# w_in's eight transfers held until unit 1's k has landed, in a kernel of a gated recurrence and a rational MLP

## The chip, the core and the metric

The kernel runs on one core of a Trainium2 chip. The metric is the device time of one execution in microseconds (us), lower is better. Engines are named as in the profile: PE (TensorE matmuls; PEld its weight loads), DVE (VectorE), ACT (ScalarE), POOL (GpSimd), SP (SyncE). SPq and POOLq are the queues from which SP and POOL issue DMAs.

## The reference, cut to what matters

Two computations in a row. First a gated linear recurrence for 4 batches, 8 heads, 768 time steps and a head size of 48; its output, laid out as 3072 tokens by 384, is the input x of an MLP with 2048 hidden units whose activation is a quotient of polynomials.

```python
f = 1.0 / (1.0 + np.exp(-f_logit))
for t in range(S):
    state = f[:, :, t, :, None] * state + np.einsum('bhd,bhe->bhde', k[:, :, t], v[:, :, t])
    y[:, :, t] = np.einsum('bhd,bhde->bhe', q[:, :, t], state)
...
h = x @ w_in
h2 = h * h
h3 = h2 * h
P = a[0] + a[1] * h + a[2] * h2 + a[3] * h3
Q = 1.0 + np.abs(b[0]) * np.abs(h) + np.abs(b[1]) * h2
g = P / (Q + 1e-06)
return (g @ w_out).astype(np.float32)
```

q, k, v and f_logit are float32 of shape (4, 8, 768, 48); w_in is 384 by 2048 and w_out 2048 by 384.

## The kernel before

The work is cut into 12 units. A unit is one batch and 256 time steps (`UB` = 2 blocks of 128 tokens); units 0 to 3 are the first 256 steps of the four batches, units 4 to 7 the next, and so on, so unit 4 needs the state that unit 0 leaves. Each unit goes through a recurrence part and an MLP part, and the parts of neighbouring units overlap.

The order of all work is written out by hand in the string `ORDER`. Each entry is a step, a call of a short function: `ld 1 k` calls `load(1, "k")`. The steps are issued in that order, and each engine and each DMA queue runs its own share of them strictly in order; semaphores between engines follow from the tiles that the steps read and write. So only the order within one engine or queue matters, and an instruction that waits holds up what stands behind it on its own engine. A number with `@` is one of four PSUM slots.

The steps that matter here (line numbers of the kernel before):

- `ld n f|k|q|v` (L204): loads f_logit, k, q or v of unit n. f, k and q go out on SP's queue, v on POOL's, where it is cast to bf16. Each of f, k, q is 128 partitions by 8 runs of 384 bytes, 1024 packets; unit 0's are split into halves. Each name has three buffers (`rings(key, 3, ...)`), so unit 3 uses unit 0's again.
- `wi m0 m1` (`load_w_in`, L212): loads columns m0*128 to m1*128 of w_in, cast to bf16, in four DMAs from POOL, one for each group of 32 partitions. `wi 0 8` and `wi 8 16` together are the whole matrix, eight DMAs of 192 KB. `wo` (L219) does the same for w_out.
- `ef`, `ls` (ACT, L282 and L287) make the log gates out of f; `cs` (PE, L297 and L302) sums them; `A` (ACT, L310) exponentiates; `xa n 1` and `xa n 0` (L315, on DVE, sometimes POOL) multiply k and q by that.
- `T` (PE, L329) transposes both, `Te` copies them out of PSUM (L336); `sc` (PE, L350) makes the scores, `mk` (DVE, L358) masks them; `vm` (POOL, L365) copies parts of v; `yi` and `yb` (PE, L371) form y; `ic`, `si` (PE, L417 and L426) and `st` (DVE, L446) carry the state; `ye` (ACT mostly, L434) writes x.
- `h n m0 m1` (PE, L455) is x @ w_in for hidden blocks m0 to m1, `hy` (ACT, L467) takes it out. `sq`, `ab`, `zv`, `p1`, `p2`, `pm`, `tv`, `gm` (DVE, L471 to L533), `lz`, `ex` (ACT, L501 and L506) and the accumulating DMAs `zd` (L497) and `ta` (L525) from POOL form g.
- `o` (PE, L542) is g @ w_out, `oe` (L548) takes it out into one of two buffers `osb`, `so` (L557, SP's queue, two DMAs) stores it.

Two suffixes tie a step to a DMA: `!w` puts a mark w on the step, and `^w` makes a step's instructions wait until what carries the mark is done (`behind`). Neither is used in the kernel before.

On POOL the first steps are `ld 0 v`, `ld 1 v`, `vm 0 1`, then the eight w_in DMAs, then `vm 0 0`, `ld 3 v`, `vm 1 1`, `vm 1 0`, `ld 2 v`. On SP's queue the loads go out in this order: unit 0's halves of f, k, q with unit 1's f among them, then `ld 2 f`, `ld 1 k`, `ld 1 q`, `ld 2 q`, `ld 3 f`, `ld 2 k`, `ld 4 f`, `ld 4 q`, `ld 3 q`.

Of the kernel before, what the change touches and what calls it, by code (L numbers as in the profile page):

```python
# [25 lines left out]
si 1 0 @3; ic 1; yi 0 1 @2; st 1 0; yb 0 2 4; Te 1; yb 0 0 2; ld 4 f; sc 1 0 @1; ye 0 s; ld 3 v; sc 1 1 @0
mk 1 0; si 1 1; vm 1 1; vm 1 0; h 0 0 4 @2; mk 1 1; ld 2 v; st 1 1; xa 2 0; h 0 4 8 @1; hy 0 0 4; ld 4 q
yi 1 1 @0; hy 0 4 8; yb 1 2 4; yb 1 0 2; ab 0 0 8; ef 3; h 0 12 16 @3; sq 0 0 8; ye 1 s; ld 3 q; ls 3
h 0 8 12 @2; zv 0 0 8; hy 0 12 16; cs 3 @1; xa 2 1; hy 0 8 12; h 1 4 8 @0; lz 0 0 8; ld 6 f; sq 0 8 16
h 1 8 12 @3; p1 0 0 16; ld 5 k; hy 1 4 8; si 2 0 @2; ab 0 8 16; A 3 0; T 2 @0; ld 3 k; pm 0 0 16; hy 1 8 12  # L30
Te 2 s; h 1 12 16 @3; ld 5 f; p2 0 0 16; ic 2; ld 5 q; ae 3; hy 1 12 16; h 1 0 4 @0; zv 0 8 16; ef 4; ta 0 8 16
ld 4 k; A 3 1; sc 2 0 @3; st 2 0; hy 1 0 4; xa 3 0; yi 2 1 @1; mk 2 0; xa 3 1 0 4 p; lz 0 8 16; sc 2 1 @0
si 2 1; mk 2 1; vm 3 1; ls 4; ic 3 @3; vm 2 1; st 2 1; vm 2 0; ex 0 0 16; ld 4 v; yb 2 2 4; sq 1 0 16; si 3 0
ta 0 0 8; yb 2 0 2; cs 4 @0; wo 12 16; ab 1 0 16; T 3 @2; wo 0 4; ae 4; vm 3 0; st 3 0; ye 2 s; wo 8 12
p1 1 0 16; si 3 1; A 4 1; h 2 0 4 @1; wo 4 8; Te 3 s; st 3 1; pm 1 0 16; h 2 4 8 @3; A 4 0; sc 3 0 @2; hy 2 4 8
u 1 12 16 @0; p2 1 0 16; hy 2 0 4; h 2 12 16 @3; ln 1 12 16; xa 4 0; ta 1 8 16; sc 3 1 @1; ef 5; mk 3 0
h 2 8 12 @0; xa 4 1 0 4 p; hy 2 12 16; mk 3 1; ls 5; yi 3 1 @2; yb 3 0 2; hy 2 8 12; gm 0 0 16; yb 3 2 4; ld 8 f
cs 5 @3; ye 3 s; ic 4 @1; ae 5; A 5 1; ab 2 0 16; h 3 8 12 @0; ef 6; A 5 0; zv 1 0 8; u 1 8 12 @2; hy 3 8 12
o 0 0 8 12 @3; sq 2 0 16; ln 1 8 12; si 4 0; h 3 4 8 @0; ls 6; lz 1 0 8; T 4 @2; p1 2 0 16; zd 2 0 8; o 0 1 0 4
st 4 0; xa 5 1 0 4 p; hy 3 4 8; Te 4; si 4 1; o 0 1 8 12; ex 1 0 16; st 4 1; sc 4 0 @0; ta 1 0 8; sc 4 1 @2  # L40
pm 2 0 16; o 0 0 12 16; zd 2 8 16; h 3 0 4 @1; ld 6 v; p2 2 0 16; o 0 0 4 8; ld 5 v; hy 3 0 4; o 0 1 4 8; ef 8
o 0 1 12 16; mk 4 1; ta 2 8 16; h 3 12 16 @1; lz 2 0 8; xa 5 0; o 0 0 0 4; vm 4 0; mk 4 0; vm 4 1; hy 3 12 16
yi 4 1 @2; yi 4 0; gm 1 0 16; yb 4 0 2; oe 0 0 2 s; yb 4 2 4; so 0 0 2; cs 6 @0; ye 4 s; ld 6 q; h 4 4 8 @1
ld 6 k; A 6 0; sq 3 0 16; lz 2 8 16; h 4 0 4 @3; ld 7 f; p1 3 0 16; ae 6; h 4 8 12 @2; hy 4 4 8; hy 4 0 4
ab 3 0 16; si 5 0 @1; ic 5; A 6 1; T 5 @3; tv 2 0 8; hy 4 8 12; zd 3 8 16; o 1 0 12 16 @0; st 5 0; ex 2 0 16
ld 7 q; o 1 0 0 4; pm 3 0 16; o 1 1 4 8; h 4 12 16 @2; ld 8 q; zv 3 0 8; o 1 0 4 8; hy 4 12 16; si 5 1
o 1 1 0 4; p2 3 0 16; o 1 1 12 16; Te 5 s; o 1 1 8 12; gm 2 0 16; ta 3 0 8; lz 3 8 16; ta 3 8 16; sc 5 1 @2
ld 7 k; sc 5 0 @3; o 1 0 8 12; vm 5 0; st 5 1; xa 6 1 0 4 p; ld 9 f; mk 5 1; o 2 0 0 4 @1; lz 3 0 8; o 2 1 12 16
mk 5 0; vm 5 1; ic 6 @2; vm 6 1; ls 8; sq 4 0 16; yi 5 0 @3; yi 5 1; oe 1 0 2 s; o 2 1 8 12; ef 7; o 2 0 4 8
ex 3 0 16; yb 5 0 2; xa 6 0; yb 5 2 4; o 2 1 4 8; ab 4 0 16; ld 8 v; si 6 0; o 2 0 12 16; p1 4 0 16; ld 7 v  # L50
T 6 @0; so 1 0 2; o 2 0 8 12; ld 8 k; ye 5 s; vm 6 0; st 6 0; zd 4 0 8; p2 4 0 16; ls 7; si 6 1; o 2 1 0 4
Te 6 s; h 5 12 16 @3; st 6 1; zv 4 8 16; cs 7 @2; oe 2 0 2 s; pm 4 0 16; h 5 0 4 @0; A 7 0; so 2 0 2; ld 10 f
hy 5 12 16; h 5 8 12 @1; hy 5 0 4; ld 11 f; gm 3 0 16; h 5 4 8 @3; ae 7; hy 5 8 12; A 7 1; sc 6 1 @0; xa 7 0
sc 6 0 @1; hy 5 4 8; cs 8 @2; mk 6 1; xa 7 1 0 4 p; lz 4 8 16; o 3 0 12 16 @3; o 3 0 8 12; mk 6 0; ta 4 0 8
T 7 @0; A 8 0; ab 5 0 16; ta 4 8 16; ld 9 k; ef 9; yi 6 1 @1; yi 6 0; o 3 1 8 12; sq 5 0 16; ae 8; A 8 1
o 3 0 4 8; Te 7 s; ld 9 q; yb 6 2 4; yb 6 0 2; p1 5 0 16; ic 7 @2; lz 4 0 8; sc 7 1 @0; si 7 0; o 3 1 4 8
ye 6 v; vm 8 0; vm 7 1; o 3 1 12 16; xa 8 1 0 4 p; ls 9; st 7 0; h 6 0 4 @1; mk 7 1; ex 4 0 16; zd 5 0 8; si 7 1
pm 5 0 16; h 6 4 8 @0; o 3 0 0 4; o 3 1 0 4; ld 10 k; vm 7 0; st 7 1; hy 6 0 4; xa 8 0; h 6 12 16 @2; ef 10
gm 4 0 16; h 6 8 12 @1; oe 3 0 2 s; hy 6 4 8; T 8 @3; zv 5 8 16; hy 6 12 16; so 3 0 2; sc 7 0 @0; hy 6 8 12
cs 9 @2; p2 5 0 16; ld 10 q; lz 5 8 16; o 4 1 8 12 @1; mk 7 0; o 4 0 8 12; ta 5 8 16; lz 5 0 8; ab 6 0 16  # L60
ta 5 0 8; yi 7 1 @0; yi 7 0; yb 7 0 2; ld 9 v; yb 7 2 4; Te 8; o 4 0 12 16; ye 7 s; vm 8 1; o 4 0 0 4; sq 6 0 16
A 9 0; o 4 1 4 8; A 9 1; sc 8 0 @3; ic 8 @0; ae 9; ex 5 0 16; sc 8 1 @2; xa 9 1 0 4 p; si 8 0; o 4 1 12 16
o 4 1 0 4; p1 6 0 16; zd 6 8 16; zd 6 0 8; ef 11; st 8 0; ld 10 v; mk 8 0; ls 10; h 7 4 8 @0; ls 11; mk 8 1
h 7 0 4 @3; xa 9 0; h 7 12 16 @2; hy 7 0 4; p2 6 0 16; hy 7 4 8; o 4 0 4 8; pm 6 0 16; h 7 8 12 @3; hy 7 12 16
cs 10 @0; hy 7 8 12; gm 5 0 16; yi 8 0 @2; ta 6 8 16; A 10 0; yi 8 1; yb 8 2 4; ae 10; yb 8 0 2; oe 4 0 2 s
T 9 @3; ye 8 s; so 4 0 2; sq 7 0 16; A 10 1; o 5 0 12 16 @1; ld 11 q; Te 9 s; si 9 0 @2; h 8 12 16 @0; ld 11 k
p1 7 0 16; o 5 0 0 4; hy 8 12 16; ic 9; ab 7 0 16; lz 6 0 8; sc 9 0 @3; sc 9 1 @0; o 5 0 4 8; tv 6 0 8
o 5 1 8 12; zd 7 0 8; lz 6 8 16; o 5 1 4 8; mk 9 1; xa 10 1 0 4 p; mk 9 0; h 8 4 8 @0; ex 6 0 16; vm 9 1
zd 7 8 16; xa 10 0; h 8 8 12 @3; vm 9 0; st 9 0; ld 11 v; p2 7 0 16; h 8 0 4 @2; pm 7 0 16; hy 8 8 12
o 5 1 12 16; o 5 1 0 4; hy 8 4 8; o 5 0 8 12; hy 8 0 4; cs 11 @3; gm 6 0 16; ta 7 8 16; oe 5 0 2 s; ic 10 @0  # L70
ta 7 0 8; A 11 0; yi 9 0 @2; yi 9 1; yb 9 2 4; A 11 1; sq 8 0 16; yb 9 0 2; ae 11; T 10 @1; ye 9 s; lz 7 0 8
si 10 0; h 9 8 12 @3; xa 11 0; ab 8 0 16; h 9 4 8 @2; hy 9 8 12; lz 7 8 16; p1 8 0 16; h 9 12 16 @3; zd 8 0 8
vm 10 0; st 10 0; vm 10 1; hy 9 4 8; Te 10; vm 11 0; o 6 0 12 16 @0; zd 8 8 16; o 6 1 4 8; hy 9 12 16; pm 8 0 16
sc 10 0 @2; ex 7 0 16; sc 10 1 @1; o 6 1 0 4; o 6 1 12 16; mk 10 0; xa 11 1 0 4 p; h 9 0 4 @3; mk 10 1
# [26 lines left out]
def kernel(  # L101
# [95 lines left out]
    def load(n, what, a0=0, a1=HP, qu="s"):  # L197
# [6 lines left out]
        return eng.dma_start(out=s[what][:, hh].rearrange("p h i d -> p h (i d)"),  # L204
                      in_=src[s["b"], hh, t0:t0 + NT, :].rearrange("h (p i) d -> p h (i d)", i=2))
# [404 lines left out]
```

## Time and profile before

| | |
|---|---|
| time, median of 3 runs | 233.66 us (233.58 to 235.81) |
| the profiled execution's own time | 234.32 us |
| its span, first to last instruction | 232.6 us |
| PE / DVE / ACT / POOL busy | 197.3 / 204.8 / 195.9 / 85.2 us |
| w_in's DMAs issued | from 8.97 us, 4.43 us for all eight |
| unit 1's k issued | at 6.66 us, its issue took 2.80 us |
| DVE's longest idle stretch | 5.67 us, ended by the landing of unit 1's k |

The times of instructions count from the start of the span. The row of a DMA instruction is its issue on the queue, not the transfer; when the data is there is seen in the landing, and in when a waiting instruction starts. What a row has in brackets is the idle time of the engine ahead of it and what ended it.

### The profile page before, as it was taken

To read this page: it belongs to the slowest core of one execution; us is meant where nothing else is said; L and a number is where in the kernel's file an instruction comes from. 1 tells how busy PE (TensorE), PEld (TensorE's weight loads), DVE (VectorE), ACT (ScalarE), POOL (GpSimd) and SP (SyncE) were. 2 spreads that over 40 slices of the span, in tenths; PEclk is the share of its full clock that TensorE was granted. 3 is DMA by queue.
4 is the path that set the end of the run, shared out by engine and by line. 5 is a ranking of instruction groups with operands and counts; after the bars stand their busy time and mean duration, and the time that the engine had idled before them with its cause. 6 is when DMAs were issued, how large, how long until landed. Compare 5 with 4: busy or idle time off the path is not lost.

```text
span 232.6 us, 6998 instructions
## 1 busy us (share of the span) xinstructions
PE 197.3 (85%) x3109; PEld 143.0 (61%) x3112; DVE 204.8 (88%) x184; ACT 195.9 (84%) x183; POOL 85.2 (37%) x104
## 2 busy tenths in 40 slices
...
DVE  5261788999999999999999999999999999979960
...
GB/s 143 220 233 232 260 179 86 246 194 146 179 219 133 159 178 270 263 239 247 264 216 243 175 169 189 163 197 206 165 148 77 158 186 201 207 207 135 91 72 131
DMA packets 61822, 43.18 MB, mean 186 GB/s; under 512 B 51424, under 2 KB 56544, under 8 KB 61792
## 3 DMA queue, kind: packets, MB, share of 16 engines
...
HBM read 25.17 MB, written 4.72 MB: 128 GB/s over the span
## 4 chain that ended last, share of the span: by engine, by line
DVE 42%; PE 22%; DMA 16%; issue 8%; ACT 6%; SPq 4%; POOL 0%; DVEq 0%; ACTq 0%
PE op L542 10%; PE hp L455 8%; DVE scm L358 7%; DMA q<-in_q_dram 7%; DVE h L471 6%; DMA g<-hy 5%; DMA z<-h 5%; DVE g L533 5%; DVE g L521 4%; SPq L204 4%; DVE hy L516 3%; DVE g L511 3%; DVE z L475 3%; DVE qkp L315 3%; DVE state L446 2%
## 5 line engine op out<-in xcount | busy, mean ns | idle before, releaser
L455 PE MATMUL hp<-x,w_in_sb 128*128 128x256 bf16 x576 | 69.8, 278 | 5.8 <-ACT x L434 2.5
L542 PE MATMUL op<-w_out_sb,g 128*128 128x384 bf16 x384 | 68.9, 326 | 0.1
L455 PEld LDWEIGHTS <-w_in_sb 128*128 128x128 bf16 x576 | 57.0, 100 | 18.2 <-issue 7.7
L467 ACT CAST hy<-hp 128x1024 bf16<-128x1024 f32 x48 | 49.4, 1081 | 6.5 <-PE hp L455 6.5
L542 PEld LDWEIGHTS <-g 128*128 128x128 bf16 x384 | 36.3, 98 | 23.7 <-issue 1.1
L501 ACT ACTIVATE lq<-z 128x2048 f32<-128x2048 bf16 x22 | 43.0, 1972 | 3.0 <-DMA z<-h 3.0
L506 ACT ACTIVATE qi<-lq 128x4096 bf16<-128x4096 f32 (+1 forms) x14 | 44.4, 3178 | 0.1
L525 POOL DMA_DIRECT2D g<-hy x19 | 18.7, 1174 | 52.6 <-DVE hy L516 21.6
L497 POOL DMA_DIRECT2D z<-h x16 | 15.6, 978 | 42.0 <-ACT lq L501 9.0
L521 DVE TENSOR_TENSOR g<-g,h 128x4096 bf16<-128x4096 bf16 (+1 forms) x13 | 29.4, 2262 | 0.0
L358 DVE TENSOR_TENSOR scm<-sc,mask 128x1024 bf16<-128x1024 f32 x24 | 28.4, 1214 | 1.0 <-PE sc L350 1.0
L533 DVE TENSOR_TENSOR g<-g,qi 128x4096 bf16<-128x4096 bf16 (+1 forms) x14 | 27.7, 1980 | 1.5 <-ACT qi L506 0.8
L471 DVE TENSOR_TENSOR h<-hy 128x4096 bf16<-128x4096 bf16 (+1 forms) x13 | 27.7, 2129 | 1.4 <-ACT hy L467 1.3
L310 ACT ACTIVATE A<-cs 128x768 f32<-128x768 f32 (+1 forms) x26 | 20.4, 808 | 8.8 <-DVE qkp L315 8.8
L204 POOL DMA_DIRECT2D v<-in_v_dram x12 | 15.8, 1372 | 20.4 <-PE y L371 17.0
L315 POOL TENSOR_TENSOR qkp<-k,A 128x768 bf16<-128x768 f32 x9 | 19.3, 2146 | 6.7 <-ACT A L310 6.7
L329 PE MATMUL tp<-ident,qkp 128*128 128x128 bf16 x192 | 14.8, 234 | 6.6 <-DVE qkp L315 6.3
L511 DVE TENSOR_SCALAR g<-hy,a_sb 128x4096 bf16<-128x4096 bf16 x12 | 18.1, 1511 | 0.1
L329 PEld LDWEIGHTS <-qkp 128*128 128x128 bf16 x192 | 12.4, 105 | 8.2 <-DVE qkp L315 6.8
L516 DVE TENSOR_SCALAR hy<-hy,a_sb 128x4096 bf16<-128x4096 bf16 x12 | 16.9, 1407 | 0.0
L315 DVE TENSOR_TENSOR qkp<-q,A 128x768 bf16<-128x768 f32 (+1 forms) x13 | 11.6, 895 | 5.8 <-ACT A L310 4.4
L365 POOL COPY vmp<-v 128x128 bf16<-128x128 bf16 x24 | 14.9, 692 | 4.8 <-DMA v<-in_v_dram 3.6
...
## 6 DMA issues: line engine op xcount, KB each, us to landing
...
```

Source lines behind the costliest of these rows:

```text
L204: return eng.dma_start(out=s[what][:, hh].rearrange("p h i d -> p h (i d)"), in_=src[s["b"], hh, t0:t0 + NT, :].rearrange("h (p i) d -> p ...
L315: i = (nc.gpsimd if eng == "p" else nc.vector).tensor_mul(s["qk"][:, x, :, hh, 0:D], s["qk"[x]][:, hh].rearrange("p h i d -> p i h d"), s[ ...
L329: nc.tensor.transpose(t[:, x, i, p, :], s["qk"][:, x, i, 2 * p:2 * p + 2, :].rearrange("t h d -> t (h d)"), ident)
L358: return nc.vector.tensor_mul(t, s["sc", g].rearrange("s r a i t -> s (r a) (i t)"), mb)
L455: nc.tensor.matmul(t[:, m - m0, :].rearrange("f (j t) -> f j t", j=UB), w_in_sb[:, kk, m * P:(m + 1) * P], s["x"][:, :, kk, :], start=(kk ...
L467: nc.scalar.copy(fl(big(s, "hy"), m0, m1), fl(s["hp", m0], 0, m1 - m0))
L471: return nc.vector.tensor_mul(fl(big(s, "h2"), m0, m1), fl(big(s, "hy"), m0, m1), fl(big(s, "hy"), m0, m1))
L501: nc.scalar.activation(fl(lq, m0, m1), fl(big(s, "z"), m0, m1), AF.Ln, scale=regs[2], bias=1.0 + 1e-6)
L506: nc.scalar.activation(fl(qi, m0, m1), fl(lq, m0, m1), AF.Exp, scale=-1.0)
L521: return nc.vector.tensor_mul(fl(big(s, "g"), m0, m1), fl(big(s, "g"), m0, m1), fl(big(s, "h2"), m0, m1))
L533: return nc.vector.tensor_mul(fl(big(s, "g"), m0, m1), fl(big(s, "g"), m0, m1), fl(qi, m0, m1))
L542: nc.tensor.matmul(s["op", g][:, j, 0:DM], big(s, "g")[:, m, C * j:C * j + C], w_out_sb[:, m, :], start=(s["on", j] == 1), stop=(s["on", j ...
```

## The change

1. `ld 1 k` gets the mark w, and `load_w_in` issues one DMA in place of four, so that `ORDER` names the eight DMAs one by one. Each has `^w`: POOL issues the first of them only when unit 1's k has landed. Their sizes, sources and order among themselves stay.
2. On POOL, `vm 0 0` goes out ahead of the eighth w_in DMA; before it came after it. All other POOL steps keep their order.
3. On SP's queue `so 5` (the store of unit 5's output) stands ahead of `so 6`; before it stood behind it. All other SP steps keep their order.
4. On PE, DVE and ACT each engine's own sequence of steps is the same as before. The lines of `ORDER` are interleaved differently between engines, and PSUM slots 1 and 3 trade names from an early step on; in substance only `sc 0 1` and `cs 2` trade their slots.

```diff
-ab_ a a; ld 1 k; cs 0 2 4 @2; ef 1; A 0 0 0 2; A 0 1 0 2; A 0 1 2 4; ae 0 0 2; A 0 0 2 4; ls 1; xa 0 0 2 4
-ld 1 q; xa 0 0 0 2; ae 0 2 4; cs 1 @3; xa 0 1 2 4; xa 0 1 0 2; T 0 2 4 @1; ae 1; A 1 0; ld 2 q; vm 0 1; wi 0 8
-ic 0; A 1 1; Te 0 2 4; T 0 0 2 @2; ef 2; st 0 0; ld 3 f; si 0 1; ls 2; Te 0 0 2; sc 0 1 @1; wi 8 16; st 0 1
-ld 2 k; cs 2 @3; xa 1 1; xa 1 0; sc 0 0 @2; A 2 1; fb; vm 0 0; T 1 @0; A 2 0; mk 0 0; ae 2; fr; mk 0 1
...
+ab_ a a; cs 0 2 4 @2; ef 1; ld 1 k !w; vm 0 1; A 0 0 0 2; A 0 1 0 2; A 0 1 2 4; ae 0 0 2; A 0 0 2 4; ls 1
+xa 0 0 2 4; ae 0 2 4; cs 1 @3; ld 1 q; xa 0 0 0 2; xa 0 1 2 4; ld 2 q; ae 1; A 1 0; xa 0 1 0 2; T 0 2 4 @1
+A 1 1; ld 3 f; ic 0; Te 0 2 4; ef 2; T 0 0 2 @2; st 0 0; ls 2; ld 2 k; si 0 1; wi 0 0 8 ^w; Te 0 0 2; sc 0 1 @3
+wi 1 0 8 ^w; st 0 1; cs 2 @1; wi 2 0 8 ^w; xa 1 1; ld 4 f; wi 3 0 8 ^w; xa 1 0; wi 0 8 16 ^w; sc 0 0 @2; A 2 1
+wi 1 8 16 ^w; fb; T 1 @0; A 2 0; mk 0 0; wi 2 8 16 ^w; ld 4 q; ae 2; fr; vm 0 0; wi 3 8 16 ^w; mk 0 1; si 1 0 @1
...
-so 6 0 2; vm 11 1; mk 11 0; o 7 0 0 4; so 5 0 2; ex 8 0 16; zd 9 8 16; h 10 4 8 @0; pm 9 0 16; h 10 12 16 @2
...
+cs 11 @1; gm 6 0 16; ta 7 8 16; oe 5 0 2 s; ic 10 @0; ta 7 0 8; A 11 0; so 5 0 2; yi 9 0 @2; yi 9 1; yb 9 2 4
...
-    def load_w_in(m0, m1):
-
-        n = (m1 - m0) * P
-        made = []
-        for a in range(HP):
-            made.append(nc.gpsimd.dma_start(out=w_in_sb[32 * a:32 * a + 32, :, m0 * P:m1 * P],
-                                in_=bass.AP(tensor=moe_w_in.tensor,
-                                            offset=moe_w_in.offset + 96 * a * d_ff + m0 * P,
-                                            ap=[[d_ff, 32], [32 * d_ff, KD], [1, n]])))
-        return made
+    def load_w_in(a, m0, m1):
+
+        return nc.gpsimd.dma_start(out=w_in_sb[32 * a:32 * a + 32, :, m0 * P:m1 * P],
+                            in_=bass.AP(tensor=moe_w_in.tensor,
+                                        offset=moe_w_in.offset + 96 * a * d_ff + m0 * P,
+                                        ap=[[d_ff, 32], [32 * d_ff, KD], [1, (m1 - m0) * P]]))
```

More of the change, by code (lines that the diff above doesn't have):

```diff
@@ L19 @@
 ORDER = """
-ab_ b a; ld 0 f 0 2; cz 1; cu 0; ld 0 f 2 4; cz 3; cz 2; cz 0; ld 0 k 0 2; cu 1; ld 1 f; ld 0 q 2 4; ld 0 v; cm
-ld 0 q 0 2; fa; ci; ef 0 0 2; ld 0 k 2 4; ld 1 v; si 0 0 @0; ef 0 2 4; ld 2 f; ls 0 0 2; ls 0 2 4; cs 0 0 2 @1
-ab_ a a; ld 1 k; cs 0 2 4 @2; ef 1; A 0 0 0 2; A 0 1 0 2; A 0 1 2 4; ae 0 0 2; A 0 0 2 4; ls 1; xa 0 0 2 4
-ld 1 q; xa 0 0 0 2; ae 0 2 4; cs 1 @3; xa 0 1 2 4; xa 0 1 0 2; T 0 2 4 @1; ae 1; A 1 0; ld 2 q; vm 0 1; wi 0 8
-ic 0; A 1 1; Te 0 2 4; T 0 0 2 @2; ef 2; st 0 0; ld 3 f; si 0 1; ls 2; Te 0 0 2; sc 0 1 @1; wi 8 16; st 0 1
@@ L25 @@
-ld 2 k; cs 2 @3; xa 1 1; xa 1 0; sc 0 0 @2; A 2 1; fb; vm 0 0; T 1 @0; A 2 0; mk 0 0; ae 2; fr; mk 0 1
[L26 to L74, printed above, removed]
@@ L75 @@
-o 6 0 4 8; hy 9 0 4; p2 8 0 16; yb 10 2 4 @2; lz 8 0 8; yb 10 0 2; T 11 @1; gm 7 0 16; ta 8 0 8; yi 10 1
-yi 10 0; ta 8 8 16; o 6 0 0 4; ye 10 s; o 6 0 8 12; Te 11 s; sq 9 0 16; o 6 1 8 12; o 7 1 12 16 @3; lz 8 8 16
-o 7 0 12 16; ab 9 0 16; h 10 8 12 @2; p1 9 0 16; oe 6 0 2 s; zd 9 0 8; sc 11 0 @1; hy 10 8 12; o 7 0 4 8
-so 6 0 2; vm 11 1; mk 11 0; o 7 0 0 4; so 5 0 2; ex 8 0 16; zd 9 8 16; h 10 4 8 @0; pm 9 0 16; h 10 12 16 @2
-h 10 0 4 @1; p2 9 0 16; hy 10 12 16; o 7 1 8 12; hy 10 4 8; gm 8 0 16; ta 9 0 8; si 11 0 @2; hy 10 0 4; ic 11
@@ L80 @@
-ta 9 8 16; sc 11 1 @0; o 7 1 4 8; lz 9 0 8; st 11 0; yi 11 0 @1; mk 11 1; yi 11 1; yb 11 0 2; lz 9 8 16
-ab 10 0 16; yb 11 2 4; o 7 1 0 4; sq 10 0 16; o 7 0 8 12; ye 11 s; o 8 1 0 4 @2; ex 9 0 16; o 8 1 8 12
-h 11 0 4 @0; p1 10 0 16; zd 10 0 8; zd 10 8 16; h 11 12 16 @1; oe 7 0 2 v; pm 10 0 16; so 7 0 2; h 11 4 8 @3
-hy 11 0 4; hy 11 12 16; h 11 8 12 @0; hy 11 4 8; p2 10 0 16; o 8 1 12 16; hy 11 8 12; gm 9 0 16; o 8 0 8 12
-ta 10 8 16; lz 10 0 8; o 8 1 4 8; o 8 0 4 8; sq 11 0 16; o 9 1 0 4 @1; ex 10 0 8; o 9 1 8 12; o 9 0 0 4
@@ L85 @@
-lz 10 8 16; o 8 0 0 4; ab 11 0 16; o 8 0 12 16; tv 10 0 8; u 11 0 4 @3; zd 11 8 16; oe 8 0 2 s; u 11 4 8 @0
-p1 11 0 16; ln 11 0 4; so 8 0 2; o 9 1 12 16; ln 11 4 8; gm 10 0 8; o 9 0 8 12; ex 10 8 16; o 9 0 12 16
-pm 11 0 8; o 10 1 4 8 @2; o 9 0 4 8; p2 11 0 16; ex 11 0 8; o 10 0 4 8; o 9 1 4 8; gm 10 8 16; o 10 0 0 4
-oe 9 0 2 s; tv 11 0 8; lz 11 8 16; o 10 1 12 16; so 9 0 2; o 10 0 12 16; gm 11 0 8; o 10 1 8 12; ex 11 8 16
-o 10 1 0 4; pm 11 8 16; o 11 1 0 4 @3; o 11 0 0 4 @0; tv 11 8 16; o 11 1 4 8; o 10 0 8 12; gm 11 8 16
@@ L90 @@
-o 11 0 4 8; oe 10 0 2 s; o 11 1 12 16; so 10 0 2; o 11 1 8 12; o 11 0 12 16; oe 11 1 2 v; o 11 0 8 12; so 11 1 2
-oe 11 0 1 s; so 11 0 1
+ab_ b a; ld 0 f 0 2; cz 1; cu 0; ld 0 f 2 4; cz 3; cz 2; cz 0; ld 0 k 0 2; cu 1; ld 1 f; ld 0 v; cm; ld 0 q 2 4
+ci; ld 0 q 0 2; ld 1 v; ef 0 0 2; si 0 0 @0; ld 0 k 2 4; fa; ef 0 2 4; ls 0 0 2; ld 2 f; ls 0 2 4; cs 0 0 2 @1
+ab_ a a; cs 0 2 4 @2; ef 1; ld 1 k !w; vm 0 1; A 0 0 0 2; A 0 1 0 2; A 0 1 2 4; ae 0 0 2; A 0 0 2 4; ls 1
+xa 0 0 2 4; ae 0 2 4; cs 1 @3; ld 1 q; xa 0 0 0 2; xa 0 1 2 4; ld 2 q; ae 1; A 1 0; xa 0 1 0 2; T 0 2 4 @1
@@ new lines @@
+A 1 1; ld 3 f; ic 0; Te 0 2 4; ef 2; T 0 0 2 @2; st 0 0; ls 2; ld 2 k; si 0 1; wi 0 0 8 ^w; Te 0 0 2; sc 0 1 @3
+wi 1 0 8 ^w; st 0 1; cs 2 @1; wi 2 0 8 ^w; xa 1 1; ld 4 f; wi 3 0 8 ^w; xa 1 0; wi 0 8 16 ^w; sc 0 0 @2; A 2 1
+wi 1 8 16 ^w; fb; T 1 @0; A 2 0; mk 0 0; wi 2 8 16 ^w; ld 4 q; ae 2; fr; vm 0 0; wi 3 8 16 ^w; mk 0 1; si 1 0 @1
+ic 1; yi 0 1 @2; st 1 0; yb 0 2 4; Te 1; yb 0 0 2; sc 1 0 @3; ye 0 s; ld 3 v; sc 1 1 @0; mk 1 0; si 1 1
+h 0 0 4 @2; vm 1 1; vm 1 0; mk 1 1; ld 2 v; st 1 1; xa 2 0; h 0 4 8 @3; hy 0 0 4; ld 3 q; yi 1 1 @0; hy 0 4 8
@@ new lines @@
+yb 1 2 4; ef 3; yb 1 0 2; ab 0 0 8; h 0 12 16 @1; sq 0 0 8; ye 1 s; ls 3; zv 0 0 8; h 0 8 12 @2; hy 0 12 16
+ld 6 f; xa 2 1; cs 3 @3; hy 0 8 12; ld 5 k; h 1 4 8 @0; lz 0 0 8; sq 0 8 16; ld 3 k; h 1 8 12 @1; p1 0 0 16
+hy 1 4 8; ld 5 f; si 2 0 @2; ab 0 8 16; A 3 0; T 2 @0; pm 0 0 16; hy 1 8 12; ld 5 q; Te 2 s; h 1 12 16 @1
+ld 4 k; p2 0 0 16; ic 2; ae 3; hy 1 12 16; h 1 0 4 @0; zv 0 8 16; ef 4; ta 0 8 16; A 3 1; sc 2 0 @1; st 2 0
+hy 1 0 4; xa 3 0; yi 2 1 @3; mk 2 0; xa 3 1 0 4 p; lz 0 8 16; sc 2 1 @0; si 2 1; mk 2 1; vm 3 1; ls 4; ic 3 @1
@@ new lines @@
+vm 2 1; st 2 1; vm 2 0; ex 0 0 16; ld 4 v; yb 2 2 4; sq 1 0 16; si 3 0; ta 0 0 8; yb 2 0 2; cs 4 @0; wo 12 16
+ab 1 0 16; T 3 @2; ae 4; st 3 0; ye 2 s; wo 0 4; p1 1 0 16; si 3 1; A 4 1; h 2 0 4 @3; Te 3 s; st 3 1; vm 3 0
+wo 8 12; pm 1 0 16; h 2 4 8 @1; wo 4 8; A 4 0; sc 3 0 @2; hy 2 4 8; u 1 12 16 @0; p2 1 0 16; hy 2 0 4
+h 2 12 16 @1; ln 1 12 16; xa 4 0; ta 1 8 16; sc 3 1 @3; ef 5; mk 3 0; h 2 8 12 @0; xa 4 1 0 4 p; hy 2 12 16
+mk 3 1; ls 5; yi 3 1 @2; yb 3 0 2; hy 2 8 12; gm 0 0 16; yb 3 2 4; ld 8 f; cs 5 @1; ye 3 s; ic 4 @3; ae 5; A 5 1
@@ new lines @@
+ab 2 0 16; h 3 8 12 @0; ef 6; A 5 0; zv 1 0 8; u 1 8 12 @2; hy 3 8 12; o 0 0 8 12 @1; sq 2 0 16; ln 1 8 12
+si 4 0; h 3 4 8 @0; ls 6; lz 1 0 8; T 4 @2; p1 2 0 16; zd 2 0 8; o 0 1 0 4; st 4 0; xa 5 1 0 4 p; hy 3 4 8; Te 4
+si 4 1; o 0 1 8 12; ex 1 0 16; st 4 1; sc 4 0 @0; ta 1 0 8; sc 4 1 @2; pm 2 0 16; o 0 0 12 16; zd 2 8 16
+h 3 0 4 @3; ld 6 v; p2 2 0 16; o 0 0 4 8; hy 3 0 4; o 0 1 4 8; ef 8; o 0 1 12 16; mk 4 1; ld 5 v; h 3 12 16 @3
+lz 2 0 8; ta 2 8 16; xa 5 0; o 0 0 0 4; vm 4 0; mk 4 0; vm 4 1; hy 3 12 16; yi 4 1 @2; yi 4 0; gm 1 0 16
@@ new lines @@
+yb 4 0 2; oe 0 0 2 s; yb 4 2 4; so 0 0 2; cs 6 @0; ye 4 s; ld 6 q; h 4 4 8 @3; ld 6 k; A 6 0; sq 3 0 16
+lz 2 8 16; h 4 0 4 @1; p1 3 0 16; ae 6; h 4 8 12 @2; hy 4 4 8; hy 4 0 4; ab 3 0 16; ld 7 f; si 5 0 @3; ic 5
+A 6 1; T 5 @1; tv 2 0 8; hy 4 8 12; zd 3 8 16; o 1 0 12 16 @0; ld 7 q; st 5 0; ex 2 0 16; o 1 0 0 4; pm 3 0 16
+o 1 1 4 8; ld 8 q; h 4 12 16 @2; zv 3 0 8; o 1 0 4 8; hy 4 12 16; si 5 1; o 1 1 0 4; p2 3 0 16; o 1 1 12 16
+Te 5 s; o 1 1 8 12; gm 2 0 16; ta 3 0 8; ld 7 k; lz 3 8 16; ta 3 8 16; sc 5 1 @2; sc 5 0 @1; o 1 0 8 12; ld 9 f
@@ new lines @@
+vm 5 0; st 5 1; xa 6 1 0 4 p; mk 5 1; o 2 0 0 4 @3; lz 3 0 8; o 2 1 12 16; mk 5 0; vm 5 1; ic 6 @2; vm 6 1; ls 8
+sq 4 0 16; yi 5 0 @1; yi 5 1; oe 1 0 2 s; o 2 1 8 12; ef 7; o 2 0 4 8; so 1 0 2; ex 3 0 16; yb 5 0 2; ld 8 k
+xa 6 0; yb 5 2 4; o 2 1 4 8; ab 4 0 16; ld 8 v; si 6 0; o 2 0 12 16; p1 4 0 16; ld 7 v; T 6 @0; o 2 0 8 12
+ye 5 s; st 6 0; vm 6 0; zd 4 0 8; p2 4 0 16; ls 7; si 6 1; o 2 1 0 4; Te 6 s; h 5 12 16 @1; st 6 1; zv 4 8 16
+cs 7 @2; oe 2 0 2 s; pm 4 0 16; h 5 0 4 @0; A 7 0; so 2 0 2; hy 5 12 16; h 5 8 12 @3; ld 10 f; hy 5 0 4; ld 11 f
@@ new lines @@
+gm 3 0 16; h 5 4 8 @1; ae 7; hy 5 8 12; A 7 1; sc 6 1 @0; xa 7 0; sc 6 0 @3; hy 5 4 8; cs 8 @2; mk 6 1
+xa 7 1 0 4 p; lz 4 8 16; o 3 0 12 16 @1; o 3 0 8 12; mk 6 0; ta 4 0 8; T 7 @0; A 8 0; ab 5 0 16; ef 9; ld 9 k
+yi 6 1 @3; yi 6 0; o 3 1 8 12; sq 5 0 16; ae 8; A 8 1; ta 4 8 16; o 3 0 4 8; Te 7 s; ld 9 q; yb 6 2 4; yb 6 0 2
+p1 5 0 16; ic 7 @2; lz 4 0 8; sc 7 1 @0; si 7 0; o 3 1 4 8; ye 6 v; vm 8 0; vm 7 1; o 3 1 12 16; xa 8 1 0 4 p
+ls 9; st 7 0; h 6 0 4 @3; mk 7 1; ex 4 0 16; zd 5 0 8; si 7 1; pm 5 0 16; h 6 4 8 @0; ld 10 k; o 3 0 0 4
@@ new lines @@
+o 3 1 0 4; vm 7 0; st 7 1; hy 6 0 4; xa 8 0; h 6 12 16 @2; ef 10; gm 4 0 16; h 6 8 12 @3; oe 3 0 2 s; hy 6 4 8
+T 8 @1; so 3 0 2; zv 5 8 16; hy 6 12 16; sc 7 0 @0; hy 6 8 12; cs 9 @2; p2 5 0 16; ld 10 q; lz 5 8 16
+o 4 1 8 12 @3; mk 7 0; o 4 0 8 12; ta 5 8 16; lz 5 0 8; ab 6 0 16; ta 5 0 8; yi 7 1 @0; yi 7 0; yb 7 0 2
+yb 7 2 4; Te 8; ld 9 v; o 4 0 12 16; ye 7 s; vm 8 1; o 4 0 0 4; sq 6 0 16; A 9 0; o 4 1 4 8; A 9 1; sc 8 0 @1
+ic 8 @0; ae 9; ex 5 0 16; sc 8 1 @2; xa 9 1 0 4 p; si 8 0; o 4 1 12 16; o 4 1 0 4; p1 6 0 16; zd 6 8 16; ef 11
```

27 lines of the change are left out of this document (added).

## The prediction

> **What bounds the kernel now.** I read the page first, for the shares and the slices.
>
> ```profile
> PE 197.3 (85%) x3109; PEld 143.0 (61%) x3112; DVE 204.8 (88%) x184; ACT 195.9 (84%) x183; POOL 85.2 (37%) x104
> ...
> DVE  5261788999999999999999999999999999979960
> ...
> DVE 42%; PE 22%; DMA 16%; issue 8%; ACT 6%; SPq 4%; POOL 0%; DVEq 0%; ACTq 0%
> ```
>
> From slice 8 (a slice is 5.8 us) DVE is full almost to the end. A microsecond saved on DVE behind that is paid for in work; one saved ahead of it moves the whole rest forward. So I read the first 35 us closely: the timeline of DVE, then the chain of waits.
>
> ```profile
> 22.47 0.96 DVE L315 TENSOR_TENSOR qkp<-k,A 128x768 bf16<-128x768 f32 x1 [5.67 <-DMA k<-in_k_dram]
> 24.73 0.96 DVE L315 TENSOR_TENSOR qkp<-q,A 128x768 bf16<-128x768 f32 x1 [1.30 <-DMA q<-in_q_dram]
> ```
>
> ```profile
> 6.66 2.80 SPq L204
> 9.46 0.04 issue
> 9.51 15.20 DMA q<-in_q_dram
> ```
>
> DVE stood still from 16.80 to 22.47 for unit 1's k (`xa 1 1`) and again for its q (`xa 1 0`), and the chain runs through that q for 15.20 us. Why so long, the DMA view tells: first the stretch 12.44 to 22.9, with w_in under way, then 24 to 30, without.
>
> ```profile
> DMA packets 2878, 2.34 MB, mean 223 GB/s; under 512 B 2111, under 2 KB 2111, under 8 KB 2877
> ...
> q0 software_dynamic: 893, 1.57, 79.7%
> q1 hardware_dynamic: 1984, 0.75, 33.6%
> ```
>
> ```profile
> DMA packets 4123, 1.56 MB, mean 260 GB/s; under 512 B 4123, under 2 KB 4123, under 8 KB 4123
> ```
>
> q1 carries SP's loads, 1024 packets each. Alone it passes 4123 packets in 6 us, 687 per us, so a load takes 1.49 us. Beside w_in (q0) it passes 1984 in 10.46 us. By the trace's packet records k's 1024 went from 12.44 to 19.87, 7.43 us, and the last engine's share landed at 22.38.
>
> **The change, part by part.**
>
> *w_in goes behind k.* Nothing is left on q0 after `ld 1 v` (its last packet 11.71), so k has the engines to itself: 12.44 + 1.49 = 13.93, and q 15.42. From last packet to landing other loads took 1.33 to 1.72 us (q1, q2, k2, f4, q4); with 1.6, k lands at 15.5 and q at 17.0. DVE is free at 16.80: `xa 1 1` runs 16.83 to 17.79, `xa 1 0` to 18.75, against 25.69 before, 6.94 earlier.
>
> *What then stands in the way.* PE's rows:
>
> ```profile
> 18.02 0.64 PE L350 MATMUL sc<-T 48*64 48x128 bf16 x16
> ...
> 23.49 1.03 PE L329 MATMUL tp<-ident,qkp 128*128 128x128 bf16 x8 [4.83 <-DVE qkp L315]
> ...
> 31.55 3.28 PE L455 MATMUL hp<-x,w_in_sb 128*128 128x256 bf16 x24
> ...
> 35.90 2.78 PE L455 MATMUL hp<-x,w_in_sb 128*128 128x256 bf16 x24
> ```
>
> `sc 0 0` ends at 18.66 whatever k does, and `T 1` needs two times 1.03 us, so it ends at 20.72; a pure shift of its old end, 26.77, would be 19.83. Of these 0.9 us, 0.5 were slack (`yi 0 1` ended at 28.13, `yb 0` waited for masks until 28.61): 0.4 is lost, 6.5 remains. `h 0 0 4`, the first use of w_in, would start at 31.55 - 6.5 = 25.05 and `h 0 12 16`, the first of the second half, at 29.4.
>
> *The added wait.* POOL waits for k from 9.0 to 15.5; behind it stand the eight issues (4.43 us), `vm 0 0` (0.30 us) and `ld 3 v`. `vm 0 0` ends near 20.2, `yb 0` wants it at 22.1; `ld 3 v` waits for `yb 0` anyway. No run shows w_in's delay from issue to first packet on a free queue: `ld 3 v` took 1.65 us, `ld 0 v` 3.17. I take 1.65, because that transfer too followed on a long idle queue while 3.17 was the queue's very first, so 17.15. Before, w_in's packets ran from 12.27, the fourth DMA done at 17.39 (5.12 later), the eighth at 22.92 (10.65 later), beside a full q1, as they will be again. That gives 22.3 and 27.8, and with their own landing delays of 1.2 and 0.8, 23.5 against the need at 25.05 and 28.6 against 29.4. With 3.17 it is 25.0 and 30.1: 0.7 late. So this term costs 0 to 0.7, and I take 0.
>
> *The loads now behind w_in.* q1 passed 1024 packets in 7.43 us beside w_in. q2 is through at 16.9; f3 ends near 23, k2 near 29 and lands at 30.5; `xa 2 1` wants k2 at 38.91 - 6.5 = 32.4. Then f4, q4, q3 beside two v's (2.1 to 3 us each, as f1 and q0 beside v) and f6, k5, k3 at 1.49: k3 lands near 41, its user `xa 3 1` on POOL (48.46) moves to 42. The DMA engines idled from 36.5 to 39.1; this backlog uses up that gap. 0 taken, at most 2 us late for k3.
>
> *The clock.* PE's early matmuls are slow: 1.03 us for eight transposes, where sixteen take 1.05 at 42.63. The clock also fell to 0.50 from 141.8 to 145.2, with `hp` x36 at 5.76 us there and 4.09 at 187.19: 1.7 us of PE. A kernel shifted by 6.5 us can lose this or get it elsewhere: -1.7 to +1.7, taken as 0. [...]
>
> *so 5 ahead of so 6.* Near the end, the timeline:
>
> ```profile
> 186.07 16.42 SPq L557 DMA_DIRECT2D out_dram<-osb  x6
> ...
> 186.93 0.88 POOL L497 DMA_DIRECT2D z<-h  x1
> ...
> 198.05 1.91 ACT L501 ACTIVATE lq<-z 128x2048 f32<-128x2048 bf16 x1 [3.04 <-DMA z<-h]
> ...
> 207.84 2.29 DVE L471 TENSOR_TENSOR h<-hy 128x4096 bf16<-128x4096 bf16 x1 [1.35 <-ACT hy L467]
> ```
>
> `oe 5` was done at 165.5, but its store waited behind `so 6` until 187.4 and fell into the transfer of `zd 9 8 16` (11.1 us to land, median 7.0), for which ACT then idled 3.04 us. Stores took 3.5 us of all engines' time between 186 and 198 for 511 packets; some 190 of `so 5`'s lie inside that transfer, 1.3 us. Moved to 166, they meet `ta 7 0 8` (landed 171.83, used by DVE at 179.71): slack. Bounds: -0.2 for that collision, 2.0 from DVE's idle stretches behind 198 (0.31, 1.35, 0.37). I take 1.0.
>
> *`vm 0 0` ahead of the last w_in issue* delays that one by 0.30; inside the margin. The trade of PSUM slots between `sc 0 1` and `cs 2` puts neither behind anything still busy.
>
> **Sum.** 6.5 + 1.0 = 7.5: the profiled execution's 234.32 (span 232.6 and 1.7 around it) would be 226.8. That execution lies 0.66 over the median, so 226.2 for the median.
>
> **The rivals.**
>
> *Something later eats part of it.* First packet after 3.17 (0.7), k3 late by 2, no gain from `so 5` (1.0): one to three of these give 227 to 230. For it: margins of 0.8 and 1 us. Against: the queue had a hole of 2.6 us.
>
> *Nothing gained at the start.* If k lands at 22.4 whatever w_in does, or POOL's wait ends early (k's semaphore counted an earlier transfer at 4.20), only `so 5` remains: 232.7. Against: DVE waited on that same semaphore and did not start before 22.38; q1's pace is 3.6 times higher without w_in.
>
> *w_in becomes the late one: slower.* Entering last beside six queued loads, it may be held as the v's were: `ld 1 v` took 3.78 us beside loads, a v alone 2.20, 1.7 times. The point: `h 0 12 16` started at 35.90 before; the eighth DMA lands later than that when each takes over (35.90 - 0.8 - 17.15)/8 = 2.24 us, against 1.33 before. At 1.7 times (2.27) the gain is just gone; at 3 us the eighth lands at 41.95, 6.05 late: 233.7 + 6.05 - 1.0 = 238.7. Against: the 1.33 was measured beside a full q1 too. [...]
>
> *More than forecast:* the half clock does not recur and `so 5` gives 2.0: 223.5.
>
> **How the numbers follow.** Forecast 0.60 (its own range 224.3 to 228.0); part eaten 0.17; more 0.08; nothing gained 0.09; slower 0.06. A measurement of this kernel tells about 1%, 2.3 us: the first three lie below 231.3, so faster 0.85, same 0.09, slower 0.06. The range runs from 223.6, the gain with all extras, to 230.6, where the part-eaten case ends.
>
> **What would show it.** Right: POOL's first w_in issue at 15.5, not 8.97; `xa 1 1` starts at 16.8 with no DMA ahead of it; `h 0 0 4` near 25; no ACT wait of 3 us for z near 190; DVE's busy time unchanged at 205. Wrong: an idle PE ahead of `h 0 0 4` or `h 0 12 16` ended by w_in's DMA; `xa 3 1` waiting for k; k landing after 17.

## The result and the profile after

The changed kernel takes 226.68 us (median of 4 executions, 225.72 to 228.66), against 234.74 (233.58 to 236.10) for the kernel before beside it: ratio 0.9665, 95% interval 0.9569 to 0.9762. The profiled execution took 227.22 with a span of 225.5, 7.1 us less than the profiled execution of before. Measured again beside later runs, the ratio was 0.9718 (0.9662 to 0.9774), so the gain is some 3%, by the two intervals 2.3 to 4.3%.

The page shows where it went: the busy times are the same to within 1.7 us, and DVE reaches its full slices earlier. In the slices of the clock two new dips stand near the start.

```profile
PE 195.6 (87%) x3109; PEld 141.4 (63%) x3112; DVE 203.9 (90%) x184; ACT 195.7 (87%) x183; POOL 84.9 (38%) x104
...
DVE  5279649999999999999999999999999999999960
...
PEclk9999589969999999999999999999999999999998
...
DVE 40%; ACT 16%; PE 16%; DMA 12%; issue 11%; SPq 2%; POOL 1%; DVEq 0%; ACTq 0%
```

DVE's timeline: unit 1's k and q are there when DVE comes free at 15.9, and the waits of 5.67 and 1.30 us are gone. In their place stands one of 5.01, later.

```profile
15.87 0.95 DVE L311 TENSOR_TENSOR qkp<-k,A 128x768 bf16<-128x768 f32 x1
16.73 0.95 DVE L311 TENSOR_TENSOR qkp<-q,A 128x768 bf16<-128x768 f32 x1
...
31.41 0.69 DVE L471 TENSOR_SCALAR z<-hy 128x2048 uint16<-128x2048 uint16 x1 [5.01 <-ACT hy L463]
```

POOL's timeline has the hold: w_in's first issue at 15.33 in place of 8.97. PE's has the new wait and a slow first stretch of `h`.

```profile
15.33 3.88 POOL L209 DMA_DIRECT2D w_in_sb<-in_moe_w_in_dram  x7 [6.17 <-DMA k<-in_k_dram]
```

```profile
25.79 4.54 PE L451 MATMUL hp<-x,w_in_sb 128*128 128x256 bf16 x24 [2.31 <-DMA w_in_sb<-in_moe_w_in_dram]
```

The chain of waits now runs through w_in where it ran through unit 1's q:

```profile
6.43 8.61 DMA k<-in_k_dram
15.04 0.28 issue
15.33 1.66 POOL w_in_sb L209 x3
16.99 8.67 DMA w_in_sb<-in_moe_w_in_dram
25.66 0.14 issue
25.79 4.55 PE hp L451 x24
```

Since DVE, ACT and PE run the same instructions in the same order in both kernels, the lead can be read step by step, as the start before less the start after of the same instruction:

| instruction | before | after | lead, us |
|---|---|---|---|
| `xa 1 1` (DVE) | 22.47 | 15.87 | 6.6 |
| `xa 1 0` (DVE) | 24.73 | 16.73 | 8.0 |
| `ye 0`, x for the first `h` (ACT) | 30.16 | 21.59 | 8.6 |
| first matmul of `h 0 0 4` (PE) | 31.55 | 25.79 | 5.8 |
| `ab 0 0 8` (DVE) | 35.91 | 31.41 | 4.5 |
| `gm 4` (DVE) | 126.57 | 121.45 | 5.1 |
| `zd 9 8 16` issued (POOL) | 186.93 | 181.23 | 5.7 |
| the Ln that waits for it (ACT) | 198.05 | 190.95 | 7.1 |

So 8.6 us were won by the time x was ready and 4.1 of them given back within the first two `h` steps. The rest of the 7.1 comes late: 1.2 on the way through the middle and 1.4 at the store.

### The profile page after: what moved, and what is told of

The parts are those of the page before. It is cut to its first block, busy times and chain, and to the rows that moved or that the text cites. A ratio compares the mean times of both kernels' runs of the same rounds, so it can differ in the third digit from the quotient of the medians.

```text
span 225.5 us, 6998 instructions
## 1 busy us (share of the span) xinstructions
PE 195.6 (87%) x3109; PEld 141.4 (63%) x3112; DVE 203.9 (90%) x184; ACT 195.7 (87%) x183; POOL 84.9 (38%) x104
## 4 chain that ended last, share of the span: by engine, by line
DVE 40%; ACT 16%; PE 16%; DMA 12%; issue 11%; SPq 2%; POOL 1%; DVEq 0%; ACTq 0%
PE op L538 9%; DVE h L467 6%; DVE g L529 5%; DVE scm L354 5%; PE hp L451 5%; DVE g L517 5%; DMA z<-h 4%; ACT lq L497 4%; ACT hy L463 4%; DMA w_in_sb<-in_moe_w_in_dram 4%; DMA k<-in_k_dram 4%; DVE g L507 4%; DVE z L471 3%; ACT qi L502 3%; DVE z L489 3%
## 5 line engine op out<-in xcount | busy, mean ns | idle before, releaser
L451 PEld LDWEIGHTS <-w_in_sb 128*128 128x128 bf16 x576 | 56.6, 99 | 18.7 <-issue 9.3
L521 POOL DMA_DIRECT2D g<-hy x19 | 18.7, 1173 | 55.0 <-DVE hy L512 24.9
L517 DVE TENSOR_TENSOR g<-g,h 128x4096 bf16<-128x4096 bf16 (+1 forms) x13 | 29.4, 2258 | 0.0
L471 DVE TENSOR_SCALAR z<-hy 128x4096 uint16<-128x4096 uint16 (+1 forms) x13 | 14.7, 1134 | 5.0 <-ACT hy L463 5.0
L204 POOL DMA_DIRECT2D v<-in_v_dram x12 | 14.9, 1296 | 6.6 <-issue 3.5
L367 PE MATMUL y<-scm,v 64*32 64x128 bf16 x384 | 12.4, 225 | 3.4 <-DVE scm L354 3.3
L293 PE MATMUL cs<-lsp,Ui 128*128 128x384 bf16 (+1 forms) x39 | 11.3, 352 | 4.3 <-ACT lsp L283 4.2
```

The costliest lines, as they stand in the source:

```text
L451: nc.tensor.matmul(t[:, m - m0, :].rearrange("f (j t) -> f j t", j=UB), w_in_sb[:, kk, m * P:(m + 1) * P], s["x"][:, :, kk, :], start=(kk ...
L471: return nc.vector.tensor_scalar(fl(big(s, "z"), m0, m1).bitcast(U16), fl(big(s, "hy"), m0, m1).bitcast(U16), 0x7FFF, None, op0=ALU.bitwis ...
L517: return nc.vector.tensor_mul(fl(big(s, "g"), m0, m1), fl(big(s, "g"), m0, m1), fl(big(s, "h2"), m0, m1))
```

## The experiments

Theory: the hold frees unit 1's k and q, the start is then set by w_in's landing and by PE's clock, and the early store of unit 5 is a second, separate gain. Rivals: the new order of steps, not the hold, makes the start; the clock alone is what the start lacks; w_in is late because of the loads it now shares the engines with; the shorter wait at the end is only the shifted start. Ratios are to the kernel before, beside each run; the diffs are against the changed kernel.

**The store without the hold.**

```diff
-ld 1 k !w;
+ld 1 k;
...
-wi 0 0 8 ^w;
+wi 0 0 8;
```

(and the same for the other seven)

> The changed kernel without the wait for unit 1's k, all eight w_in DMAs issued from about 9 us on: the early store alone. If the hold makes the start, DVE waits some 6 and 1.3 us for unit 1's k and q again, the first matmul of h starts near 31.5, and the time is 232 to 233, 1.0 to 1.5 below the kernel before. If the other order of the steps made the start, k lands near 15 here too and the time stays near 226.5.

Ratio 0.9920 (0.9889 to 0.9951), 232.12 us against 233.74: 0.8% less, which is 1.9 us, a little over what was expected (1.6 by the medians). The timeline of DVE has the waits back:

```profile
18.71 0.96 DVE L311 TENSOR_TENSOR qkp<-k,A 128x768 bf16<-128x768 f32 x1 [2.51 <-DMA k<-in_k_dram]
24.99 0.96 DVE L311 TENSOR_TENSOR qkp<-q,A 128x768 bf16<-128x768 f32 x1 [5.32 <-DMA q<-in_q_dram]
```

k came at 18.7 here and not near 22.4, perhaps because it was further through when w_in's packets began (the author's estimate), and for q DVE waited the longer, 5.32 us in place of 1.30; together 7.8 us, as before (7.0). The hold makes the start, and the order of the steps does not: the first `h` starts at 31.81 here, 31.55 in the kernel before. And with the early store ACT's wait is shorter with no shift of the start at all, 1.65 us where it had been 3.04:

```profile
198.18 1.91 ACT L497 ACTIVATE lq<-z 128x2048 f32<-128x2048 bf16 x1 [1.65 <-DMA z<-h]
```

The profiled execution itself, at 234.48 us, was no faster than that of the kernel before: its first `h` lost 1.1 us to the half clock (4.39 us for 24 matmuls against 3.28).

**The hold without the store.**

```diff
-A 11 0; so 5 0 2; yi 9 0 @2;
+A 11 0; yi 9 0 @2;
...
-so 6 0 2; mk 11 0; o 7 0 0 4;
+so 6 0 2; mk 11 0; o 7 0 0 4; so 5 0 2;
```

> The changed kernel with so 5 behind so 6 again: the hold of w_in alone. If the early store is worth what the prediction took for it (1.0 us, bounds -0.2 to 2.0), the landing of the second zd 9 takes some 11 us again instead of 9.7, ACT waits about 3 us for it instead of 1.6, and the time is 1.0 to 1.5 us above the changed kernel, 227.5 to 228. If the shorter wait came from the shifted start alone, the time stays within 0.5 us of the changed kernel's.

228.25 us, ratio 0.9747 (0.9683 to 0.9812): above the changed kernel's two ratios, 0.9665 and 0.9718, by 0.7 to 1.9 us, but the intervals overlap, so by itself this run doesn't settle the store's worth. The wait for z that was expected did not come: z landed in 8.7 us, although 410 packets of the stores began in that time (512 in the kernel before, 256 in the changed one). In the profiled execution PE's clock was halved from 173.8 to 177.3 (sixteen transposes take 1.82 us of the chain there, 1.00 in the changed kernel), and the work around `zd 9` ran later, by the author's estimate for that. But the second profile of the changed kernel (below) has the same half clock, from 174.5 to 178.0, with the early store, and there z took 9.9 us. DVE's steps in the two lie 0.2 us apart up to 191; what then sets this run 1.1 us behind is a gap on PE in the middle of `yb`, which the profile puts down to no engine and no DMA, and which was 0.58 us there:

```profile
192.98 0.28 PE L367 MATMUL y<-scm,v 64*32 64x128 bf16 x5 [1.81 <-issue]
```

So this run's profile does not show the late store making the wait for z. What the store is worth rests on the run above alone, 0.5 to 1.1% or 1.1 to 2.6 us, together with the small reorderings that that run keeps.

**PE kept busy ahead of the first h.**

```diff
-h 0 0 4 @2;
+wm 20 @2; h 0 0 4 @2;
...
+    def warm(n, sl):
+        t = slot(sl, [P, P], F32, "wm")
+        for _ in range(n):
+            nc.tensor.matmul(t, ident, ident, start=True, stop=True, skip_group_check=True)
```

> The changed kernel with 20 extra matmuls of 128 columns (identity by identity, into a PSUM tile that nothing reads) on PE ahead of the first h, where PE stood idle from 23.1 to 25.8 for w_in. If the idle PE is what keeps the clock at a half until 29.4, the stretch from 22.6 on is busy and the clock comes back near 26.0: the 24 matmuls of the first two h steps take 2.8 to 3.3 us instead of 4.54, and the time falls by 1.2 to 1.7 us to about 225.3. If the clock does not follow PE's work, or the start does not set the end, the time stays within 0.5 us of the changed kernel's. If the 20 are slower than thought (over 130 ns each) they delay h by what they take beyond 2.7 us.

225.82 us (225.35 to 226.11), ratio 0.9665 (0.9612 to 0.9717). The same 24 matmuls at full clock:

```profile
23.82 1.28 PE L563 MATMUL wm<-ident 128*128 128x128 bf16 x20
25.16 2.78 PE L451 MATMUL hp<-x,w_in_sb 128*128 128x256 bf16 x24
30.05 2.12 PE L451 MATMUL hp<-x,w_in_sb 128*128 128x256 bf16 x18 [1.01 <-DMA w_in_sb<-in_moe_w_in_dram]
```

2.78 us instead of 4.54, and DVE's next step (`ab 0 0 8`) starts at 29.02 instead of 31.41. But the second half of w_in, landing at 29.96, is now waited for by `h 0 12 16`, which gives 1.0 back: the lead over the changed kernel is 2.4 us at `ab 0 0 8` and 1.5 at `sq 0 8 16`. The granted clock by stretches, first of the changed kernel, then of this one (columns: stretch, length, busy times, then PEclk, DMA share, GB/s):

```profile
15.80:22.60 6.80, 4.68 (x177) 3.54 (x179) 6.33 (x10) 2.50 (x4) 4.21 (x9) 1.00 1.20 220
22.60:29.40 6.80, 4.49 (x43) 2.88 (x32) 3.68 (x4) 0.85 (x1) 2.28 (x4) 0.50 1.16 208
```

```profile
22.60:29.40 6.80, 5.91 (x153) 4.97 (x153) 4.49 (x6) 3.07 (x4) 2.28 (x4) 1.00 1.16 209
```

The clock was full from 19.4 on, ahead of the extra matmuls at 23.82: they can't have raised it. In the traces of the kernels before and after, each record of it but the last is a multiple of 3.41 us long (3.41, 6.83, 17.07 among them); counted on from 19.4, the step at 22.78, too, lies ahead of them; whether they kept it from falling at the next, one execution can't tell. What the run shows is the price of the half clock in the first `h`, 1.76 us of PE; that extra matmuls prevent it is not shown. The time moved by 0.9 us, the ratio is the same 0.9665, and the intervals overlap.

**The hold one load earlier.**

```diff
-ld 2 f;
+ld 2 f !w;
...
-ld 1 k !w;
+ld 1 k;
```

> The hold moved from unit 1's k to the load before it in the queue, unit 2's f, which lands at 13.54 in the changed kernel, 1.8 us ahead of the first w_in issue there. If w_in's landing is what cost the start its missing 2 us, the first packets of w_in come near 16.0, when k has passed and q nearly so, k and q land as before (15.0 and 16.6), the fourth w_in DMA lands near 23.9 instead of 25.66, h starts at 24.0 instead of 25.79 and the time falls by 1.7 us to about 225. If the half clock of PE alone is what it lacks, h starts earlier but ends no earlier, and the time stays within 0.5 us. If q is caught by w_in's packets, xa 1 0 waits for it and the time rises by 1 to 3 us.

The start came as expected: first w_in issue at 13.98, fourth landing at 23.90, PE waits 0.35:

```profile
24.04 2.78 PE L451 MATMUL hp<-x,w_in_sb 128*128 128x256 bf16 x24 [0.35 <-DMA w_in_sb<-in_moe_w_in_dram]
```

`ab 0 0 8` started at 27.90, 3.5 us ahead of the changed kernel. The time did not follow: 224.46 in one execution, 229.09, 229.87 and 230.34 in the others, the last being the profiled one. There POOL's timeline shows where the lead was lost:

```profile
43.44 1.81 POOL L311 TENSOR_TENSOR qkp<-k,A 128x768 bf16<-128x768 f32 x1 [2.51 <-DMA k<-in_k_dram]
45.19 3.83 POOL L361 COPY vmp<-v 128x128 bf16<-128x128 bf16 x3
```

Unit 3's k, the fourth load behind unit 4's q on SP's queue, landed at 43.27 and `xa 3 1` waited 2.51 us for it. POOL's next three copies took 3.83 us together where the changed kernel has 0.28 to 0.29 each: two of them took 2.36 and 1.29, beside DVE's bf16 square (from 44.53, 2.87 us) and its bitwise step (from 47.32, 1.30 us). PE waited 2.92 us for them, its clock was at 0.50 from 44.1 to 54.3, and the lead of 3.5 us became a lag of 2.9.

**The same, with unit 3's k and q ahead of unit 4's q.**

```diff
-ld 4 q; ... ld 3 q; ... ld 3 k;
+ld 3 k; ld 3 q; ... ld 4 q;
```

(the first two in the place of `ld 4 q`, that one in the place of `ld 3 q`; the hold on `ld 2 f` stays)

> The hold on unit 2's f, as in the run before, and on SP's queue unit 3's k and q ahead of unit 4's q (k of unit 3 was fourth behind it). In the run with the hold alone the start was 3.5 us ahead of the changed kernel at 28 us and then lost 6 between 47 and 55, where POOL waited 2.5 us for unit 3's k and its copies fell beside DVE's squares (2.36 and 1.29 us instead of 0.28). If the late k is what took the gain back, k lands before 38, POOL does not wait, no half clock follows at 44, the lead of some 3 us stays, and the time is near 224. If the lead is lost anyway (to unit 3's q, or to the accumulating DMAs behind the loads), the time stays at 226 or above.

224.58 us (222.49 to 224.96), ratio 0.9563 (0.9509 to 0.9616), while the changed kernel beside it had 0.9718 (0.9662 to 0.9774): faster than both kernels. Unit 3's k lands at 36.09, POOL waits only for ACT, the copies are short:

```profile
41.49 2.12 POOL L311 TENSOR_TENSOR qkp<-k,A 128x768 bf16<-128x768 f32 x1 [0.50 <-ACT A L306]
43.56 0.76 POOL L361 COPY vmp<-v 128x128 bf16<-128x128 bf16 x3
```

The granted clock stayed full from 14.9 to 223.1, and the lead of 2.5 us at `sq 0 8 16` was kept to the end (span 223.2).

**The changed kernel again,** beside that run and the next.

> The changed kernel itself once more, beside the next two on one chip: 226 to 227, h starts 25.5 to 26.0 after a wait for w_in of 2 to 2.5 us.

227.49 us, a little above what was expected but within the spread of the first time; `h` starts at 25.42 after a wait of 1.89 for w_in, and its 24 matmuls take 5.28 us with the clock halved from 24.3 to 31.2.

**w_in with little beside it.**

```diff
-A 1 1; ld 3 f; ic 0;
+A 1 1; ic 0;
...
-ls 2; ld 2 k; si 0 1;
+ls 2; si 0 1;
...
-xa 1 1; ld 4 f; wi 3 0 8 ^w;
+xa 1 1; wi 3 0 8 ^w !z; ld 3 f ^z; ld 2 k; ld 4 f;
```

> The changed kernel with SP's loads from unit 3's f on held until the fourth w_in DMA has landed, so that w_in's first half goes through with little beside it (only the end of unit 2's q). If the loads slow w_in, its four DMAs of the first half land 1 us apart or less and the fourth lands near 23 instead of 25.66, h starts with it; if w_in goes at its own pace whatever is beside it, the fourth lands at 25 to 25.7 as before. Either way unit 3's f comes later, near 28 to 29, and the loads behind it by some 5 us, so k of unit 3 comes late by more than in the run with the hold on unit 2's f: the time is 227 to 230, above the changed kernel.

228.10 us, ratio 0.9753 (0.9716 to 0.9789). The DMA view from 17 to 23: w_in has the engines, SP's queue 56 packets.

```profile
q0 software_dynamic: 484, 0.86, 101.7%
q1 hardware_dynamic: 56, 0.02, 1.4%
```

w_in's fourth DMA landed at 23.23 instead of 25.29 (the changed kernel beside it), the third and the fourth 0.96 and 0.88 us behind the one before, and only 0.45 us after the first of the engines had reported its share. `h` started at 23.41 with no wait. So some 2 us of w_in's lateness is the loads beside it: 0.2 in the first issue, 0.8 up to the first packet, 0.7 in the passage of the four DMAs and 0.4 up to the landing. But ACT then waited 3.85 us for unit 3's f, and DVE 3.56 for unit 2's k, which took the lead back (4.1 us ahead of the changed kernel at `ab 0 0 8`, 0.2 at `sq 0 8 16`):

```profile
31.09 0.84 ACT L278 ACTIVATE f<-f 128x768 f32<-128x768 f32 x1 [3.85 <-DMA f<-in_f_logit_dram]
```

## Why the prediction was right, point by point

The time, 226.2, was 0.5 us from the median, and the total in the profiled execution was forecast at 7.5 and came to 7.1. The terms fitted less well than the sum: w_in's landing cost what was put at nothing, and the middle and the store gave more than was forecast. That these misses cancel is luck.

**k and q freed: right, and larger.** k passed in 12.49 to 13.85 by the packet records, 1.36 us as against 1.49 forecast, and DVE was at `xa 1 1` at 15.87 instead of the forecast 16.83. Nearly all of the difference is DVE's own earlier start: `st 0 1` ended at 15.95 instead of 16.80, since the last of unit 0's q and k landed at 10.10 and 11.56 instead of 11.12 and 12.41. The change leaves those loads as they were, and in the seven other profiles `st 0 1` ended at 16.2 to 16.7, so this part is the spread from execution to execution. PE lost nothing at `T 1`: its eight transposes took 0.62 us instead of the 1.03 taken from the row of before, because the clock was up from 15.8 on (see below).

**w_in's landing: the term that was mis-sized.** It was put at 0 to 0.7 us and taken as 0. The fourth DMA was to land at 23.5 (25.0 at the late bound), and landed at 25.66:

| | forecast | measured |
|---|---|---|
| first issue | 15.5 | 15.33 |
| to the first packet | 1.65 (bound 3.17) | 2.47 |
| four DMAs pass | 5.12 | 6.19 |
| to the landing | 1.2 | 1.67 |

By the prediction's own list this is a sign of being wrong: PE idle ahead of `h 0 0 4`, ended by w_in's DMA. Each small step was taken from a favourable row, and the bound was laid on one of them alone. From first packet to first packet the first two DMAs took 2.42 and 1.50 us, not 1.73 and 1.13. The loads alone can't be what makes these two slow, for with little beside w_in they took 1.79 and 2.09; but over all the steps the run with w_in alone puts some 2 us down to the loads. x was also ready earlier than forecast, so the need moved forward while w_in moved back: the forecast margin of 1.5 us became a wait of 2.31 on PE. "w_in becomes the late one" was named as a rival, but priced at the second half alone and by the point where the whole gain is gone; that it might take a third of the start's gain was missed. Issued later, w_in was waited for, those 2.31 us; on the whole the hold paid all the same, since without it the kernel takes 0.9920 of the time before and with it 0.9665 and 0.9718.

**The clock: the step held at 0 with -1.7 to +1.7.** Both ends came: the half clock at 141.8 did not recur, and new ones came at 22.6 to 29.4 and 46.5 to 49.9. The first cost 1.26 us in the first 24 matmuls (4.54 against 3.28 in the kernel before; 1.76 against the full clock). It came although PE was busy for 4.68 of the 6.80 us ahead of it, and for 1.74 of the last 3.41; what sets it off is not shown. A warning on reading the clock: the profile has no record of it before it first rises and shows it as full until then, from 12.0 to 32.5 in the kernel before. The rows tell otherwise: in the changed kernel eight transposes take 1.03 us ahead of the first record and 0.62 behind it. By the records it rose at 32.5 in the kernel before and at 15.8 in the changed one.

**The middle: not forecast.** 1.2 us of lead were added between 35 and 187, 0.6 by `gm 4`, which no longer waited for its accumulating DMA, and 0.5 around the half clock that had been at 141.8. That is within what these kernels vary by from execution to execution, and was not tested.

**The store: right in size, its cause not settled.** 1.0 was taken; the wait for z fell from 3.04 to 1.64 and the lead grew by 1.4, and without the hold the store alone gave 0.5 to 1.1%. But from issue to landing z took 8.4 to 10.0 us in the seven profiles with the early store, and 11.1 and 8.7 in the two with the late one: that the late store's packets held it up is argued, and the one test of it with the hold did not show it.

**The loads behind w_in: right for this kernel, and close.** Unit 3's k was to land near 41 for a need at 42; it landed at 42.2 and its user started at 43.97. With another 1.8 us of lead it would have been late, as the run with the earlier hold showed.

So the start gave 4.5 us and not 6.5, and 1.2 in the middle with 0.4 more at the store made up for most of it.
